# Second tiles for raw weights and weight parts, and part stores issued from ScalarE

## The chip, the cores and the metric

The kernel runs on one core of a Trainium2 chip. The metric is device time in microseconds (us), the median over runs of the whole program. Times inside the program are counted from its first profiled instruction.

## The reference

Three computations follow each other. The first is an attention in two steps: 32 packed queries per head attend to keys and values, and the 576 queries of each of 8 batches attend to that packed result, in 8 heads of 64. The second and third are products with weights, over 4608 tokens:

```python
a = x @ w1
b = x @ w2
h = a * b @ w3
x = h @ w_out                     # 512 wide again
h = x @ w_in                      # 512 -> 2048
g = where(h >= 1, h, where(h <= -1, 0, (h + 1) ** 2 / 4))
out = g @ w_out2                  # 2048 -> 512
```

The weights arrive as 64-bit floats.

## The kernel before

The kernel has three stages. In the first (to about 170 us) the weights of the second computation are read and converted, and the attention of batches 0 and 1 is done. In the second stage a loop over batches b = 1 to 7 (line 675) multiplies batch b with its weights, while the attention of batch b + 1 is spread over the same instructions. In the third stage (from about 654 us, line 803 on) the third computation runs over nine blocks of tokens.

One batch of the second stage is 24 units, u = 0 to 23: sixteen `ab_unit` (line 367, 12 matmuls on L377 each) and eight `x2_unit` (line 413, 24 matmuls on L401 each). Behind each unit come up to two more things, in this order: a step of the next batch's attention (the list EARLY and LATE, lines 39 and 40, say behind which units), and in batches 1 to 6 one weight task, taken from the list `w_todo` (lines 699 to 702). The order in which the code emits instructions is the order on each engine.

The weight tasks prepare the weights of the third stage: 32 blocks of 128x512 64-bit words (16 of `win`, 16 of `wout`). A conversion task (`w_convert`, line 572) turns a raw block in SBUF into 32-bit floats (ScalarE L123, VectorE L128, L130, L134), and then issues the load of the next raw block from SyncE's queue (`load_weight`, line 106, L109). There is one raw tile (`bufs=1`). A part task (`w_parts`, line 581) splits one converted block into a rounded high part (ScalarE L585) and the rest (GpSimd L586), and issues the store of both, 512 KB, to DRAM from SyncE's queue (L587). The two parts lie in one tile `hl`, of which there is one (`bufs=1`). A combining task (L591) adds or subtracts two converted blocks on GpSimd. A line of tasks always takes three units, and a part task is always its first: parts start at units that are multiples of 3. There are 44 part tasks and 138 tasks with the empty ones. The third stage reads the stored parts back (`wi_load`, `wo_load`).

SyncE's queue also holds the large attention loads: the queries of the next batch are issued behind u = 3 (`load_q`, L157), the values and the small packed queries of the batch after behind u = 10 (`load_v`, L168 and L169, `load_p`, L162), the keys behind u = 14 (`load_k`, L152). Each load stands ahead of the weight task of the same unit. ScalarE's queue already issues the stores of the second stage's results (L429, 72 of them).

The conversions fall behind these units (b.u): 1.0, 1.1, 1.2, 1.3, 1.20, 1.22; 2.1, 2.2, 2.4, 2.7, 2.10, 2.13; 3.5, 3.7, 3.10, 3.11, 3.13, 3.16, 3.19, 3.22; 4.14, 4.16, 4.19, 4.20, 4.22; 5.1, 5.4, 5.7, 5.23; 6.1, 6.4, 6.5.

Of the kernel before, what the change touches and what calls it, by code (L numbers as in the profile page):

```python
# [8 lines left out]
F32 = mybir.dt.float32  # L9
F32R = mybir.dt.float32r  # L10
# [12 lines left out]
P = 128  # L23
# [33 lines left out]
def fused_kernel(ctx: ExitStack, tc, qT, kT, vv, pb, w1, w2, w3T, wo, win, wout, out):  # L57
    nc = tc.nc
# [22 lines left out]
    cv = tc.alloc_tile_pool(name="cv0", bufs=1, side="left", reuse_waits="tile")  # L81
# [24 lines left out]
    def load_weight(pool, src, bufs=1):  # L106

        t = pool.tile([P, 512], src.dtype, name="raw", tag="raw", bufs=bufs)
        nc.sync.dma_start(out=t, in_=src)  # L109
        return t  # L110

    def as_float32(pool, raw, out, bufs=1):

        if raw.dtype == F32:
            return lambda: None, lambda: None, lambda: nc.vector.tensor_copy(out=out, in_=raw)
        quarters = raw.bitcast(U16).rearrange("p (n four) -> p n four", four=4)
        t = pool.tile([P, 512], F32, name="cvt", tag="cvt", bufs=bufs)
        halves = out.bitcast(U16).rearrange("p (n two) -> p n two", two=2)  # L120

        def scale():
            nc.scalar.activation(  # L123
                out=t, in_=raw.bitcast(F32).rearrange("p (n two) -> p n two", two=2)[:, :, 1],
                func=AF.Copy, scale=2.0 ** -112)

        def parts():
            nc.vector.tensor_scalar(  # L128
                out=halves[:, :, 0], in0=quarters[:, :, 1], scalar1=13, scalar2=None, op0=ALU.logical_shift_right)
            nc.vector.tensor_scalar(  # L130
                out=halves[:, :, 1], in0=quarters[:, :, 3], scalar1=0x8000, scalar2=None, op0=ALU.bitwise_and)

        def join():
            nc.vector.scalar_tensor_tensor(  # L134
                out=out.bitcast(I32), in0=t.bitcast(I32), scalar=3, in1=out.bitcast(I32),
                op0=ALU.logical_shift_left, op1=ALU.bitwise_or)
        return scale, parts, join
# [214 lines left out]
    def emit(step):  # L352
        pe, ew = step
        if pe:
            pe()
        ew()
# [77 lines left out]
    raw = {}  # L434
# [120 lines left out]
    cv = tc.alloc_tile_pool(name="cv1", bufs=1, side="left", reuse_waits="tile")  # L555
# [9 lines left out]

    wx = {}
    w_todo = []

    def w_raw(src):
        raw["w"] = load_weight(cv, src)  # L570

    def w_convert(key, nxt):
        def f():
            x = wx[key] = cv.tile([P, 512], F32, name="cvx", tag="cvx", bufs=4)
            for f in as_float32(cv, raw.pop("w"), x):
                f()
            if nxt is not None:
                w_raw(nxt)
        return f

    def w_parts(key, dst):
        def f():
            x = wx[key]
            p = cv.tile([P, 2, 512], F32R, name="hl", tag="hl", bufs=1)
            nc.scalar.activation(out=p[:, 0], in_=x, func=AF.Copy)  # L585
            nc.gpsimd.tensor_tensor(out=p[:, 1], in0=x, in1=p[:, 0].bitcast(F32), op=ALU.subtract)  # L586
            nc.sync.dma_start(out=dst, in_=p.bitcast(F32))  # L587
        return f

    def w_combine(key, a, b, op):  # L590
        return lambda: nc.gpsimd.tensor_tensor(out=wx[key], in0=wx[a], in1=wx[b], op=op)  # L591

    def weight_tasks():

        groups = [(k, n) for n in range(2) for k in range(2)]
        seq = []
        for x, (k, n) in enumerate(groups):
            for r, c in ((0, 0), (1, 1), (1, 0), (0, 1)):
                seq.append(win[(2 * c + k) * P:(2 * c + k + 1) * P, (2 * r + n) * 512:(2 * r + n + 1) * 512])
            for j in range(4 * x, 4 * x + 4):  # L600
                r = (j % 2) * 8 + j // 2
                seq.append(wout[r * P:(r + 1) * P, :])
        conv = [lambda: w_raw(seq[0])]
        nxt = seq[1:] + [None]
        conv = []
        for x in range(4):
            for q in (11, 22, 21, 12):
                conv.append(w_convert((x, q), nxt[len(conv)]))
            for j in range(4 * x, 4 * x + 4):
                conv.append(w_convert(("o", j), nxt[len(conv)]))  # L610
        lines = [[conv.pop(0) for _ in range(3)], [conv.pop(0)]]
        for x, (k, n) in enumerate(groups):
            q = {z: (x, z) for z in (11, 12, 21, 22)}
            take = lambda m=1: [conv.pop(0) for _ in range(m) if conv]
            part = lambda i, z: w_parts(q[z], wid[i][n][:, k])
            lines.append([part(A11, 11), None, None])
            lines.append([part(A22, 22), w_combine(q[22], q[21], q[22], ALU.add), None])
            lines.append([part(A12, 12), None, None])
            lines.append([part(S1, 22), w_combine(q[22], q[22], q[11], ALU.subtract),
                          w_combine(q[21], q[11], q[21], ALU.subtract)])  # L620
            lines.append([part(S2, 22), w_combine(q[12], q[12], q[22], ALU.subtract)] + take())
            lines.append([part(S3, 21)] + take())
            lines.append([part(S4, 12)] + take() + take())
            for j in range(4 * x, 4 * x + 4):
                lines.append([w_parts(("o", j), wod[j // 2][:, j % 2])] + take())
        out = []
        for l in lines:
            out += (l + [None, None, None])[:3]
        assert not conv
        w_raw(seq[0])  # L630
        return out

    raw.clear()
    w_todo += weight_tasks()
    assert len(w_todo) <= 144, len(w_todo)

    wi_t, wo_t = {}, {}

    def wi_load(i, n):
        t = wi_t[i, n] = late["b1" if i in LEFT else "b2"].tile([P, 2, 2, 512], F32R, name=f"wi{i}{n}")  # L640
        nc.sync.dma_start(out=t.bitcast(F32), in_=wid[i][n])
# [4 lines left out]
    def x2_load(t):  # L646
        f = late["b1"].tile([P, 4, TB], F32, name="f", tag="f", bufs=1)
        t0 = t * TB
        nc.sync.dma_start(out=f, in_=x2d[t0 // XD][:, :, t0 % XD:t0 % XD + TB])
        for r in range(2):  # L650
            for c in range(2):
                x2f[10 * r + c + 11] = f[:, 2 * r:2 * r + 2, c * TH:(c + 1) * TH]
# [12 lines left out]
    def x2_tasks(t):  # L665

        return [
            x2_parts(t, A11, 11), x2_combine(11, 12, 11), x2_combine(12, 22, 12),
            x2_parts(t, S1, 11), x2_parts(t, A12, 21),
            x2_parts(t, S4, 22), x2_combine(22, 22, 11),  # L670
            x2_parts(t, S2, 22), x2_combine(21, 21, 22),
            x2_parts(t, S3, 12), x2_parts(t, A22, 21),
        ]

    for b in range(1, B):
        if b + 1 < B:
            att, sa, bm = attention(b + 1)
            spread = dict(zip(EARLY, att))
            spread.update(zip(LATE, [bm[1, 0], bm[0, 0], sa[0], sa[1], bm[1, 1], bm[0, 1]]))
        else:  # L680
            spread = {}
            b1 = late["b1"] = tc.alloc_tile_pool(name="b1", bufs=1, side="left", reuse_waits="tile")
            x2_load(0)
            for n in range(2):
                for i in LEFT:
                    wi_load(i, n)
            x2_todo = x2_tasks(0)
        seq = []
        for f, n in ((ab_unit, 8), (x2_unit, 4)):
            seq += [f(b, mt, hf) for hf in range(2) for mt in range(n)]  # L690
        for u, unit in enumerate(seq):
            emit(unit)
            if u in spread:
                emit(spread[u])
            if b == B - 1:
                for _ in range(2 if u >= 18 else 0):
                    if x2_todo:
                        x2_todo.pop(0)()
            elif w_todo:
                task = w_todo.pop(0)  # L700
                if task:
                    task()
        if b == B - 2:
            cv.release()
            a2.release()
# [205 lines left out]
```

## Time and profile before

| what | value |
|---|---|
| median of 3 runs | 1424.65 us (1422.08 to 1431.35) |
| the profiled execution | 1425.31 us |
| its span, first to last instruction | 1423.5 us |
| TensorE (PE) busy | 1335.9 us, 94% of the span |
| VectorE (DVE) busy | 801.6 us, 56% |
| ScalarE (ACT) busy | 618.3 us, 43% |
| GpSimd (POOL) busy | 129.4 us, 9% |
| mean granted TensorE clock, as a share of full speed | 0.978 |

The profiled execution lies within the spread of the runs. Its span leaves 1.8 us around the program's instructions. A busy matmul can be a slowed one: busy time alone doesn't say that TensorE ran at its peak.

### The profile page before, as it was taken

To read this page: it belongs to the slowest core of one execution; us is meant where nothing else is said; L and a number is where in the kernel's file an instruction comes from. 1 tells how busy PE (TensorE), PEld (TensorE's weight loads), DVE (VectorE), ACT (ScalarE), POOL (GpSimd) and SP (SyncE) were. 2 spreads that over 40 slices of the span, in tenths; PEclk is the share of its full clock that TensorE was granted. 3 is DMA by queue.
4 is the path that set the end of the run, shared out by engine and by line. 5 is a ranking of instruction groups with operands and counts; after the bars stand their busy time and mean duration, and the time that the engine had idled before them with its cause. 6 is when DMAs were issued, how large, how long until landed. Compare 5 with 4: busy or idle time off the path is not lost.

```text
span 1423.5 us, 23629 instructions
## 1 busy us (share of the span) xinstructions
PE 1335.9 (94%) x9576; PEld 1163.8 (82%) x9576; DVE 801.6 (56%) x1480; ACT 618.3 (43%) x1272; POOL 129.4 (9%) x102
## 2 busy tenths in 40 slices
PE   6689789889699999999999999999999999999998
PEld 2367678778588888898988989898898989989897
DVE  4784556655556665534555555656555555555553
ACT  3344243434254534334344444544444453444533
POOL 0000012112012121001000000001000000100000
PEclk9899999999799999999999999999999999999999
DMA  9762445544445544347324243333434233242332
GB/s 280 238 227 92 142 145 155 184 156 166 152 159 180 201 149 160 126 181 302 141 96 167 93 148 119 119 123 115 148 111 153 93 131 136 93 174 89 126 111 89
DMA packets 58878, 212.56 MB, mean 149 GB/s; under 512 B 5777, under 2 KB 17041, under 8 KB 45713
## 3 DMA queue, kind: packets, MB, share of 16 engines
q1 hardware_dynamic: 43216, 190.99, 39.0%
q10 hardware_dynamic: 15552, 20.06, 3.9%
q8 instruction: 75, 1.23, 0.4%
q14 instruction: 35, 0.28, 0.1%
HBM read 167.90 MB, written 43.12 MB: 148 GB/s over the span
## 4 chain that ended last, share of the span: by engine, by line
PE 68%; DVE 11%; DMA 10%; ACT 5%; issue 2%; POOL 1%; SPq 1%; ACTq 1%; DVEq 0%; POOLq 0%
PE o L795 24%; PE x L765 13%; PE psk L401 9%; PE psk L377 9%; PE z L765 6%; PE y L765 3%; DMA raw<-wout 2%; DMA wi<-hl 2%; DMA raw<-w3T 2%; DMA raw<-win 1%; PE psk L193 1%; DVE g L103 1%; PE psk L485 1%; DMA wo<-hl 1%; ACT r L778 1%
## 5 line engine op out<-in xcount | busy, mean ns | idle before, releaser
L795 PE MATMUL o<-wo,g 128*128 128x512 f32 x1728 | 441.3, 391 | 1.3 <-ACT g L102 1.3
L795 PEld LDWEIGHTS o<-wo,g 128*128 128x128 f32 x1728 | 304.7, 188 | 48.5 <-ACT g L102 1.7
L765 PEld LDWEIGHTS x<-x2s,wi 128*128 128x128 f32 x1728 | 243.2, 189 | 36.4 <-ACT m L773 12.4
L765 PE MATMUL x<-x2s,wi 128*128 128x256 f32 x1728 | 252.1, 282 | 7.7 <-ACT m L773 5.3
L401 PEld LDWEIGHTS psk<-g,w 128*128 128x128 f32 x1500 | 206.9, 194 | 36.9 <-ACT st L428 24.6
L401 PE MATMUL psk<-g,w 128*128 128x288 f32 x1500 | 215.2, 303 | 12.9 <-ACT st L428 8.4
L377 PE MATMUL psk<-at,m 128*128 128x288 f32 x1494 | 217.6, 302 | 5.7 <-DVE at L328 1.9
L377 PEld LDWEIGHTS psk<-at,m 128*128 128x128 f32 x1494 | 203.9, 191 | 20.9 <-issue 8.6
L779 DVE TENSOR_TENSOR H<-H,r 128x512 f32<-128x512 f32 x144 | 99.7, 692 | 182.5 <-ACT r L778 182.5
L102 ACT ACTIVATE g<-H 128x512 fp32r<-128x512 f32 x144 | 90.6, 629 | 108.6 <-DVE H L780 108.4
L778 ACT ACTIVATE r<-H,half 128x512 f32<-128x512 f32 x144 | 104.2, 724 | 66.3 <-DVE H L831 64.0
L765 PE MATMUL z<-x2s,wi 128*128 128x256 f32 x864 | 125.0, 281 | 0.0
L103 DVE TENSOR_TENSOR g<-H,g 128x512 fp32r<-128x512 f32 x144 | 103.6, 720 | 29.8 <-ACT g L102 29.8
L655 POOL TENSOR_TENSOR f<-f 128x512 f32<-128x512 f32 x36 | 49.2, 1367 | 699.9 <-DVE x2s L662 698.5
L765 PEld LDWEIGHTS z<-x2s,wi 128*128 128x128 f32 x864 | 112.0, 191 | 0.0
L389 DVE TENSOR_TENSOR tb<-psk,ta 128x288 f32<-128x288 f32 x124 | 56.4, 455 | 90.5 <-ACT ta L387 42.2
L586 POOL TENSOR_TENSOR hl<-cvx,hl 128x512 fp32r<-128x512 f32 x44 | 57.5, 1307 | 498.9 <-ACT hl L585 266.5
L780 DVE SCALAR_TENSOR_TENSOR H<-r,H 128x512 f32<-128x512 f32 x144 | 99.7, 692 | 4.9
L123 ACT ACTIVATE cvt<-raw 128x512 f32<-128x512 f32 x72 | 48.6, 678 | 89.3 <-DMA raw<-wout 31.3
L103 DVE TENSOR_TENSOR g<-tb,g 128x288 fp32r<-128x288 f32 x128 | 74.7, 583 | 17.5 <-ACT g L102 16.8
L485 PE MATMUL psk<-wo,w3f 128*128 128x512 f32 x128 | 61.9, 636 | 14.2 <-DVE w3f L134 14.2
L662 DVE TENSOR_TENSOR x2s<-f,x2s 128x512 fp32r<-128x512 f32 x63 | 46.8, 765 | 37.7 <-ACT x2s L661 37.7
(85 smaller groups left out, 1122.1 us busy)
## 6 DMA issues: line engine op xcount, KB each, us to landing
wo<-wo SPq DMA_DIRECT2D x72, 1024.0 KB, 4.8
wi<-hl SPq DMA_DIRECT2D x28, 512.0 KB, 2.6
wi<-wi SPq DMA_DIRECT2D x14, 1024.0 KB, 6.9
x2d<-st ACTq DMA_DIRECT2D x72, 144.0 KB, 1.8
qk<-kT SPq DMA_DIRECT2D x8, 1152.0 KB, 7.0
qk<-qT SPq DMA_DIRECT2D x8, 1152.0 KB, 5.9
f<-x2d SPq DMA_DIRECT2D x9, 1024.0 KB, 7.5
out<-st ACTq DMA_DIRECT2D x36, 256.0 KB, 2.7
```

The source lines that it names most:

```text
L102: nc.scalar.activation(out=dst[:, 0], in_=src, func=AF.Copy)
L103: nc.vector.tensor_tensor(out=dst[:, 1], in0=src, in1=dst[:, 0].bitcast(F32), op=ALU.subtract)
L377: nc.tensor.matmul(ps[w][:, :HS], m_tile[b, w, n][:, s, G, c0 * P:(c0 + 1) * P], at_tile[b][:, G, v, hf * HS:(hf + 1) * HS], start=(k == 0 ...
L389: nc.vector.tensor_tensor(out=g, in0=ps[0][:, :HS], in1=bs, op=ALU.mult)
L401: nc.tensor.matmul(ps, w34[kt][:, s, mt * P:(mt + 1) * P], g_t[kt, hf][:, v, :], start=(kt == kts[0] and n == 0), stop=(kt == kts[-1] and ...
L485: nc.tensor.matmul(acc[4 * hf + m], w3f[hf, j][:, m * P:(m + 1) * P], wof[j], start=(j == 0), stop=(j == 7))
L586: nc.gpsimd.tensor_tensor(out=p[:, 1], in0=x, in1=p[:, 0].bitcast(F32), op=ALU.subtract)
L765: nc.tensor.matmul(bank[b], wi_t[q, n][:, k, s, c0 * P:(c0 + 1) * P], x2_t[t, q][:, v, k, :], start=(j == 0 and q in (A11, S1, A12)), stop ...
L778: nc.scalar.activation(out=r, in_=src, func=AF.Relu, scale=0.5, bias=half)
L779: nc.vector.tensor_tensor(out=src, in0=src, in1=r, op=ALU.max)
L780: nc.vector.scalar_tensor_tensor(out=src, in0=r, scalar=1.0, in1=src, op0=ALU.min, op1=ALU.mult)
L795: nc.tensor.matmul(acc[c], g2_t[t, i, h][:, s, c * P:(c + 1) * P], wo_t[i][:, h, v, :], start=(i == 0 and h == 0 and n == 0), stop=(i == 7 ...
```

## The change

The raw block and the part tile get two tiles each. The first two raw blocks are loaded at the start, and each conversion issues the load of the block after the next. The store of a part is not issued by the part task, but put on a list; one unit later, behind that unit's attention step and ahead of its weight task, it is issued from ScalarE's queue. The 8 KB per partition that this takes come from a smaller scratch for dynamic DMAs.

```diff
-    def w_raw(src):
-        raw["w"] = load_weight(cv, src)
+    w_stores = []
+    raws = []
 
     def w_convert(key, nxt):
         def f():
             x = wx[key] = cv.tile([P, 512], F32, name="cvx", tag="cvx", bufs=4)
-            for f in as_float32(cv, raw.pop("w"), x):
+            for f in as_float32(cv, raws.pop(0), x):
                 f()
             if nxt is not None:
-                w_raw(nxt)
+                raws.append(load_weight(cv, nxt, 2))
 
     def w_parts(key, dst):
         def f():
             x = wx[key]
-            p = cv.tile([P, 2, 512], F32R, name="hl", tag="hl", bufs=1)
+            p = cv.tile([P, 2, 512], F32R, name="hl", tag="hl", bufs=2)
             nc.scalar.activation(out=p[:, 0], in_=x, func=AF.Copy)
             nc.gpsimd.tensor_tensor(out=p[:, 1], in0=x, in1=p[:, 0].bitcast(F32), op=ALU.subtract)
-            nc.sync.dma_start(out=dst, in_=p.bitcast(F32))
+            w_stores.append(lambda: nc.scalar.dma_start(out=dst, in_=p.bitcast(F32)))
...
-        conv = [lambda: w_raw(seq[0])]
-        nxt = seq[1:] + [None]
+        nxt = seq[2:] + [None, None]
...
-        w_raw(seq[0])
+        for src in seq[:2]:
+            raws.append(load_weight(cv, src, 2))
...
             elif w_todo:
+                for f in w_stores:
+                    f()
+                w_stores.clear()
                 task = w_todo.pop(0)
...
-    nc = bacc.Bacc("TRN2", target_bir_lowering=False, num_devices=1)
+    nc = bacc.Bacc("TRN2", target_bir_lowering=False, num_devices=1, dynamic_dma_scratch_size=4096)
```

## Rows read from the trace of the kernel before

**Rows 1.** Batches 1 to 6: length, busy PE, PEld, DVE, ACT, POOL; clock; DMA share, GB/s.
```profile
172.05:249.70 77.65, 67.79 (x591) 59.89 (x590) 49.00 (x95) 33.29 (x75) 13.57 (x10) 0.93 0.47 148
249.70:324.29 74.59, 64.94 (x590) 57.00 (x589) 42.55 (x86) 31.73 (x73) 11.66 (x9) 0.98 0.49 172
324.29:404.87 80.58, 65.54 (x590) 57.95 (x589) 46.16 (x91) 32.88 (x75) 14.70 (x11) 0.89 0.47 159
404.87:473.47 68.60, 65.54 (x589) 58.20 (x589) 42.99 (x83) 31.47 (x72) 16.04 (x12) 0.95 0.52 172
473.47:537.75 64.28, 62.77 (x590) 55.60 (x589) 39.68 (x79) 30.37 (x70) 15.54 (x12) 1.00 0.53 175
537.75:603.34 65.59, 63.22 (x590) 55.64 (x589) 38.68 (x77) 29.36 (x69) 8.01 (x6) 1.00 0.38 135
```

**Rows 2.** TensorE's timeline, its idle times of batches 1 to 6.
```profile
192.29 1.96 PE L232 MATMUL psm<-ident,big 128*116 128x128 f32 x8 [4.55 <-ACT big L216]
...
236.14 4.76 PE L401 MATMUL psk<-g,w 128*128 128x288 f32 x24 [2.57 <-ACT st L428]
...
264.12 1.09 PE L232 MATMUL psm<-ident,big 128*116 128x128 f32 x8 [2.30 <-ACT big L216]
...
297.35 8.03 PE L401 MATMUL psk<-g,w 128*128 128x288 f32 x48 [4.48 <-ACT ta L387]
...
312.06 3.44 PE L401 MATMUL psk<-g,w 128*128 128x288 f32 x24 [1.26 <-ACT st L428]
...
369.29 1.22 PE L193 MATMUL psm<-qk,ppt 64*32 64x288 f32 x16 [15.04 <-DVE big L295]
...
458.77 5.92 PE L401 MATMUL psk<-g,w 128*128 128x288 f32 x24 [3.06 <-ACT st L428]
...
525.52 3.44 PE L401 MATMUL psk<-g,w 128*128 128x288 f32 x24 [1.51 <-ACT st L428]
```

**Rows 3.** All engines' timeline, ScalarE's waits for a raw block or a part tile.
```profile
188.19 0.68 ACT L123 ACTIVATE cvt<-raw 128x512 f32<-128x512 f32 x1 [3.24 <-DMA raw<-win]
...
227.39 0.63 ACT L585 ACTIVATE hl<-cvx 128x512 fp32r<-128x512 f32 x1 [7.83 <-DMA wi<-hl]
...
270.69 0.64 ACT L585 ACTIVATE hl<-cvx 128x512 fp32r<-128x512 f32 x1 [2.05 <-DMA wo<-hl]
...
296.33 0.67 ACT L123 ACTIVATE cvt<-raw 128x512 f32<-128x512 f32 x1 [10.14 <-DMA raw<-win]
...
366.05 0.67 ACT L123 ACTIVATE cvt<-raw 128x512 f32<-128x512 f32 x1 [15.42 <-DMA raw<-wout]
```

**Rows 4.** The same timeline, SyncE's queue around the value load of batch 2.
```profile
278.31 4.82 SPq L169 DMA_DIRECT2D v<-vv  x1
...
283.98 0.49 SPq L109 DMA_DIRECT2D raw<-win  x1
```

**Rows 5.** All instructions on L169 (values): issue time in ns, time to landing.
```profile
L169 SPq DMA_DIRECT2D v<-vv x8: 2852/4648/4863, 18.8 to 497.6; - x8
...
DMA to landing us min/median/max: 16.3/18.8/20.4
```

**Rows 6.** Instructions on the tile hl: durations in ns, minimum, median and maximum.
```profile
L585 ACT ACTIVATE hl<-cvx x44: 612/623/635, 196.6 to 578.4; 128x512 fp32r<-128x512 f32 x44
L586 POOL TENSOR_TENSOR hl<-cvx,hl x44: 1274/1290/1579, 197.3 to 579.1; 128x512 fp32r<-128x512 f32 x44
...
DMA to landing us min/median/max: 2.6/2.7/12.0
```

**Rows 7.** All instructions on L429 (stores from ScalarE's queue).
```profile
L429 ACTq DMA_DIRECT2D x2d<-st x72: 326/326/760, 98.5 to 654.6; - x72
...
DMA to landing us min/median/max: 1.7/1.8/7.9
```

**Rows 8.** The queues' timeline around the first value load of batch 1.
```profile
102.59 4.86 SPq L169 DMA_DIRECT2D v<-vv  x1
...
106.90 0.33 ACTq L429 DMA_DIRECT2D x2d<-st  x1
```

## The prediction

> **What bounds the kernel now.** TensorE is busy for 94% of the span, so the first question is where the rest is. A table by stretch, cut at the first matmul of each batch, answers it [rows 1]. The least disturbed batch, the fifth, takes 64.28 us, and TensorE is busy for 62.77 us of it at full clock. Batch 3 holds the same matmuls and takes 80.58 us, 65.54 of it busy, at a granted clock of 0.89: there TensorE waits, and some of its busy time is slowed. I take 62.77 us as what a batch needs. The excess is then, from batch 1 to 6: 14.9, 11.8, 17.8, 5.8, 1.5 and 2.8 us, together 54.6 us. That is all that a change to the weight tasks can win: the matmuls stay as they are.
>
> The second view, TensorE's own timeline, says where the excess sits [rows 2]. Nearly all idle times are put down to ScalarE or VectorE, but these are only the messengers. ScalarE's timeline shows what they waited for [rows 3]: in batch 3 ScalarE stands 15.42 us for a raw block, and TensorE idles 15.04 us. In batch 2 it stands 10.14 us for a raw block, and TensorE idles 4.48 and then 1.26 us. In batch 1 it stands 7.83 us for the one part tile, whose store has not landed, and TensorE idles 2.57 us. A conversion or part task thus stands in ScalarE's order ahead of the copies that free TensorE's PSUM banks.
>
> The third view, SyncE's queue, says why the data is late. In batch 2 the load of values is issued at 278.31 us, its issue alone takes 4.82 us, and the raw block for the conversion at u = 13 is issued behind it at 283.98 us [rows 4]. It can be used at 296.33 us [rows 3]. The values take 16.3 to 20.4 us from issue to landing [rows 5], and what stands behind them in the queue lands with them. The stores of parts go the same way: typically 2.7 us, up to 12.0 us [rows 6].
>
> **The change part by part. Raw blocks one step earlier.** Each conversion uses a block whose load was issued two conversions before it, not one. I went through the list of tasks with this rule.
>
> Batch 1, units 0 to 3: four conversions follow each other, and the third stands 3.24 us for its block [rows 3]. The first two blocks are now loaded ahead, the third is issued one unit earlier: the wait goes. Of the idle 4.55 us behind it [rows 2] I count 2.7, since VectorE's work for the maximum of the scores follows at its own pace. The eight transposes after it took 1.96 us where those after 264.12 us took 1.09 [rows 2]: 0.9 more; for the slowed matmuls behind them I estimate twice that, 1.9. That makes 5.5 us.
>
> Batch 2: the conversion at u = 13 now uses a block issued at u = 7, ahead of the values. What goes is 4.48 us, 1.26 us, and 1.5 us of slowed matmuls (8.03 us for 48, where two times 3.44 for 24 make 6.9, and 0.4 taken for those before them), 7.2 us in sum [rows 2]. The early waits of the batch go too: 2.30 us [rows 2], and about 1.6 us of two shorter ones behind the part tile's wait of 2.05 us [rows 3]. Together 11.1 us.
>
> Batch 3: the conversion at u = 11 uses a block issued at u = 7, ahead of the values, so the 15.04 us go, and with them an estimated 2.0 us of slowed matmuls, since the clock of this batch was the lowest [rows 1], 17.0 us in all. But the next conversion, at u = 13, uses a block issued at u = 10, behind the values. That is the geometry of batch 2 before the change, so I put back its price, 7.2 us. Net 9.8 us.
>
> Batch 4: the conversion at u = 14 issues its load behind the keys, but that block is now wanted at u = 19, not at u = 16. Idle 3.06 us, and 24 matmuls in 5.92 us where 3.44 are usual [rows 2]: 5.5 us go, to which the part tile contributes.
>
> Batches 5 and 6: 1.5 us behind a wait for the part tile [rows 2], and in batch 6 the conversions at u = 4 and 5 stand close together: 2.4 of its 2.8 us.
>
> The loads are the same in number and size; 32 of them only move.
>
> **Two part tiles.** A tile is wanted again six units after its part task instead of three: 16 us at 64.28 us for 24 units [rows 1], though the shorter units come closer. With the 12.0 us of the slowest store [rows 6] nearly all such waits go. Their effect is counted in the batches above, and in batch 1 it is 4 us more: 2.57 us idle, and 1.3 us of the 4.76 us for 24 matmuls [rows 2].
>
> The sum is 5.5 + 4 + 11.1 + 9.8 + 5.5 + 1.5 + 2.4 = 39.8 us.
>
> **The stores on ScalarE's queue.** 44 store issues leave SyncE's queue, where they took as long as on ScalarE's, and where the raw, value, query and key loads stood behind their wait for GpSimd. ScalarE's issue takes 0.33 us [rows 7], so ScalarE has 44 x 0.33 = 14.5 us more to do in 430 us. What hides it is its idle time: it is busy for 30 to 33 us of each batch [rows 1]. The store also waits for GpSimd, whose subtraction takes 1.29 us behind ScalarE's copy [rows 6]. It is issued one unit later, and ahead of it stand that unit's own copies and attention step. Queued behind it on ScalarE are the conversion of the same unit and the copies of the next, and TensorE waits for these through its banks. From below this costs nothing, or gains a little where the values are issued sooner. From above, every store shows with 1.29 + 0.33 us, 71 us in all. I take 2 us, near the lower end, because a part task precedes each store by a whole unit, and even the shorter units have twelve matmuls, 1.7 us at 3.44 us for 24 [rows 2], more than the 1.29 us.
>
> A rule of the Trainium skill speaks against this part: "DMA: Bandwidth & Descriptors", section "Issuing engines are not separate DMA queues", says that transfers issued from different engines end up on the same DMA engines, so that another issuing queue saves issue time only. The trace partly agrees: a 144 KB store from ScalarE's queue typically lands in 1.8 us, but in up to 7.9 us [rows 7]. By the rule alone the moved stores land no sooner, and the second tile has to do the whole work; that is the second rival.
>
> **The scratch** issues no instruction; I cost it at nothing. Where the tiles lie moves by some KB, and a load could meet another tile's release: not seen in any row, 0 to 2 us, and I take 1 us for it and all else. With 2 us for the stores the net gain is 37 us. The profiled execution took 1425.31 us, 0.7 us above the median, so both references agree: 1425.3 - 37 gives 1388 us.
>
> **The rivals.** *The issue of the values holds ScalarE's store.* In each of batches 1 to 5 the store of the part of u = 9 comes up at u = 10, just when SyncE spends 4.6 us on issuing the values [rows 5]. If one issue excludes the other, ScalarE stands for up to 4.6 us five times. Waits of that size cost TensorE about 3 us (10.14 us cost 5.7 in idle time): 15 us, 1403 us. Against it: a ScalarE issue at 106.90 us lies inside a SyncE issue from 102.59 to 107.45 us and took the usual 0.33 us [rows 8]. "Perfetto Trace Analysis" of the Trainium skill, section "DMA Instruction — HWDGE (DVE, Sync)", describes such a lock on a shared descriptor generator; the row doesn't show one. 12%.
>
> *The stores land late and the waits for the part tile stay.* Beside the values a store shares their engines. If the store of u = 10 is not landed at u = 15, batches 1 to 5 keep a wait there; at up to the 4 us of batch 1, and 1.5 to 4 in the others, that is 14 us: 1402 us. For it: the 7.9 us of a much smaller store [rows 7]. Against it: the store has five units to land. 13%.
>
> *The third batch's wait goes too,* because SyncE issues the values sooner when no store stands before them: 7.2 us more, 1381 us. 8%.
>
> *ScalarE becomes the bound, and the kernel slower.* The store waits at the head of ScalarE's order while PSUM copies stand behind it. If all 44 show with 1.29 + 0.33 us, 71 us come on top of the 39.8 won: 1456 us. From (39.8 + 14) / 44 = 1.2 us per store on it is slower by over 1%. For it: the same messenger role of ScalarE that costs so much now. Against it: half of each batch is idle time of ScalarE. 4%.
>
> *The change does not do what it says:* the added tiles wait for their place, or the blocks stay late because the queue itself is full. Then nothing much moves, 1420 us. 4%.
>
> **How the numbers follow.** The forecast has 59%. Its own spread, from errors of the terms, is 1380 to 1396 us. The range reaches to the third batch's case below (with the remaining excess, 1425 - 54.6 = 1371 us is the floor) and to both rivals near 1403 us above: 1375 to 1405 us. Within 1%, about what a measurement can tell from no change, means 14 us: all up to 1410 us is faster. Forecast, the two rivals near 1403 and the third batch's case hold 92%; some of the two rivals, if they come together, falls into the middle. Faster 0.88, same 0.08, slower 0.04.
>
> **What would show it.** In the profile of the changed kernel batch 2 should take about 63 to 65 us, batch 3 about 70 us with one wait for a raw block at u = 13, and batch 1 about 68 us. Waits of ScalarE for the tile hl should be nearly gone. The 44 stores should show on ScalarE's queue with 0.33 us each; an issue of several us at u = 10 would show the first rival, a wait for the tile at u = 15 the second. The third stage (from 654 us on) should keep its length. The prediction is wrong if batches 2 and 3 don't shorten, or if new waits behind the stores on ScalarE come up in all six batches.

## The result and the profile after

The changed kernel takes 1390.71 us (median of 4 runs, 1388.27 to 1395.25) beside 1426.22 us of the kernel before in the same comparison: a ratio of 0.9753, with a 95% interval of 0.971 to 0.9796. Forecast were 1388 us. Its profiled execution has a span of 1386.5 us, 37.0 us less than before.

Busy time by batch, cut at the first matmul of each batch as in [rows 1] (columns: stretch, length, busy PE, PEld, DVE, ACT, POOL; clock; DMA share, GB/s):

```profile
174.55:242.19 67.64, 63.65 (x591) 55.80 (x590) 47.73 (x94) 32.56 (x75) 13.59 (x10) 1.00 0.52 177
242.19:305.81 63.62, 63.12 (x590) 55.55 (x589) 42.31 (x86) 32.03 (x73) 11.61 (x9) 1.00 0.59 201
305.81:377.61 71.80, 65.46 (x589) 58.05 (x589) 45.56 (x91) 32.84 (x75) 14.56 (x11) 0.95 0.53 179
377.61:440.31 62.70, 62.70 (x589) 55.59 (x589) 41.97 (x83) 31.48 (x72) 15.91 (x12) 1.00 0.56 188
440.31:503.00 62.69, 62.69 (x589) 55.58 (x589) 38.89 (x79) 30.23 (x70) 15.51 (x12) 1.00 0.54 179
503.00:565.71 62.71, 62.71 (x590) 55.60 (x589) 38.62 (x77) 29.66 (x69) 7.92 (x6) 1.00 0.38 132
```

In the last three batches TensorE is busy from the first matmul to the last, at full clock (granted clock 1.00). Batch 3 is the only one that still stands out. From first to last matmul cut the six batches took 431.3 us before and take 391.2 now: 40.1 us less. The span shows 37.0 of it, because the first batch starts 2.5 us later (174.55 us against 172.05) and the part behind batch 6 is 0.6 us longer. The later start is probably spread: the changed kernel run once more started its first batch at 176.0 us, and the other kernels of the table below with the same loads of values and the smaller scratch between 173.6 and 177.5 us. The kernel before was profiled once, so how far its own start moves is not shown.

TensorE's own timeline of the changed kernel, three of the seven idle times that its six batches have left (the other four are at most 1.66 us each):

```profile
191.39 1.09 PE L232 MATMUL psm<-ident,big 128*116 128x128 f32 x8 [1.50 <-ACT big L216]
...
349.03 9.02 PE L401 MATMUL psk<-g,w 128*128 128x288 f32 x48 [4.47 <-ACT ta L387]
...
365.36 3.44 PE L401 MATMUL psk<-g,w 128*128 128x288 f32 x24 [1.87 <-ACT st L428]
```

The first answers to 192.29 us in [rows 2]: 1.50 us idle instead of 4.55, and the eight transposes take 1.09 us instead of 1.96. The 15.04 us of batch 3 are gone; in their place stand 4.47 and 1.87 us, the pattern that batch 2 had before. The timeline of all engines shows what is behind it:

```profile
327.02 5.02 SPq L169 DMA_DIRECT2D v<-vv  x1
...
328.63 0.33 ACTq L586 DMA_DIRECT2D wi<-hl  x1
...
332.96 16.30 SPq L109 DMA_DIRECT2D raw<-win  x3
...
348.01 0.67 ACT L123 ACTIVATE cvt<-raw 128x512 f32<-128x512 f32 x1 [9.96 <-DMA raw<-win]
```

The second of the two loads of values (L169) is issued from 327.02 us on, the raw block for u = 13 behind them at 332.96, and ScalarE stands 9.96 us for it. The second line is a store of parts on ScalarE's queue. It is issued in the middle of the values' issue, and takes 0.33 us.

In the changed kernel the line numbers of the part task are one lower than before: ScalarE L584, GpSimd L585, store L586. ScalarE's waits from 165 us on, that is, from the table of who waited for whom (us in total, times, longest), the lines on the raw tile and the part tile, first of the kernel before, then of the changed one:

```profile
ACT cvt L123 <- DMA raw<-wout: 31.3, 7, 15.4
...
ACT hl L585 <- DMA wi<-hl: 24.9, 6, 7.8
...
ACT cvt L123 <- DMA raw<-win: 16.8, 6, 10.1
...
ACT hl L585 <- DMA wo<-hl: 6.6, 4, 3.5
```

```profile
ACT cvt L123 <- DMA raw<-win: 10.0, 1, 10.0
...
ACT cvt L123 <- POOL hl L585: 8.3, 8, 1.2
ACT ta L387 <- POOL hl L585: 7.5, 7, 1.2
```

Before, that makes 48.1 us of waits for raw blocks, in 13 pieces, and 31.5 us for the part tile, in 10. One raw wait is left, none for the part tile. New are 15.8 us in which a store on ScalarE's queue waits for GpSimd, with whoever stands behind it.

### The profile page after: what moved, and what is told of

The parts are those of the page before. It is cut to its first block, busy times and chain, and to the rows that moved or that the text cites. A ratio compares the mean times of both kernels' runs of the same rounds, so it can differ in the third digit from the quotient of the medians.

```text
span 1386.5 us, 23532 instructions
## 1 busy us (share of the span) xinstructions
PE 1327.9 (96%) x9576; PEld 1156.6 (83%) x9576; DVE 797.9 (58%) x1480; ACT 617.8 (45%) x1272; POOL 129.0 (9%) x102
## 3 DMA queue, kind: packets, MB, share of 16 engines
q1 hardware_dynamic: 36880, 167.92, 35.5%
## 4 chain that ended last, share of the span: by engine, by line
PE 77%; DVE 9%; DMA 6%; ACT 4%; issue 2%; POOL 1%; ACTq 0%; SPq 0%; DVEq 0%; POOLq 0%
PE o L797 24%; PE x L767 13%; PE psk L401 13%; PE psk L377 12%; PE z L767 6%; PE y L767 3%; DMA raw<-w3T 2%; PE psk L193 2%; DVE x2s L661 1%; DMA raw<-win 1%; PE psk L485 1%; PE psm L182 1%; ACT r L780 1%; DVE g L103 1%; DMA st<-x2d 1%
## 5 line engine op out<-in xcount | busy, mean ns | idle before, releaser
L401 PEld LDWEIGHTS psk<-g,w 128*128 128x128 f32 x1500 | 203.3, 191 | 30.2 <-ACT st L428 16.2
L401 PE MATMUL psk<-g,w 128*128 128x288 f32 x1500 | 211.7, 300 | 6.3 <-ACT ta L387 4.5
L377 PE MATMUL psk<-at,m 128*128 128x288 f32 x1494 | 213.7, 298 | 3.6 <-DVE m L103 1.7
L377 PEld LDWEIGHTS psk<-at,m 128*128 128x128 f32 x1494 | 200.6, 188 | 17.8 <-issue 7.2
L585 POOL TENSOR_TENSOR hl<-cvx,hl 128x512 fp32r<-128x512 f32 x44 | 57.4, 1305 | 461.1 <-DVE g L103 234.6
L387 ACT ACTIVATE ta<-psk 128x288 f32<-128x288 f32 x125 | 50.6, 405 | 49.8 <-PE psk L377 40.1
L103 DVE TENSOR_TENSOR g<-tb,g 128x288 fp32r<-128x288 f32 x128 | 69.8, 545 | 3.5 <-ACT g L102 2.8
```

The costliest lines, as they stand in the source:

```text
L103: nc.vector.tensor_tensor(out=dst[:, 1], in0=src, in1=dst[:, 0].bitcast(F32), op=ALU.subtract)
L377: nc.tensor.matmul(ps[w][:, :HS], m_tile[b, w, n][:, s, G, c0 * P:(c0 + 1) * P], at_tile[b][:, G, v, hf * HS:(hf + 1) * HS], start=(k == 0 ...
L401: nc.tensor.matmul(ps, w34[kt][:, s, mt * P:(mt + 1) * P], g_t[kt, hf][:, v, :], start=(kt == kts[0] and n == 0), stop=(kt == kts[-1] and ...
```

## The experiments

The table gives the length of each batch in the profiled execution of each kernel, from its first L377 matmul to the next batch's (us; such a cut lies up to 0.2 us from the one above), and the ratio to the kernel before. Kernels were compared with runs of the kernel before on the same chip, so ratios are compared, not times: the kernel before took 1426.22 us in the first comparison, 1421.67 us beside e0 to e3, 1420.88 beside e4 to e7 and 1424.26 beside e8 to e11.

| kernel | start of b1 | b1 | b2 | b3 | b4 | b5 | b6 | ratio (95% interval) |
|---|---|---|---|---|---|---|---|---|
| before | 172.1 | 77.5 | 74.6 | 80.6 | 68.6 | 64.3 | 65.6 | 1 |
| changed | 174.6 | 67.5 | 63.6 | 71.8 | 62.7 | 62.7 | 62.7 | 0.9753 (0.971 to 0.9796) |
| e0_scratch | 174.1 | 73.0 | 73.8 | 79.8 | 68.6 | 64.9 | 65.1 | 1.0012 (0.999 to 1.0034) |
| e1_raw2 | 177.0 | 69.2 | 68.9 | 72.0 | 63.9 | 63.9 | 62.7 | 0.986 (0.9838 to 0.9882) |
| e2_hl2 | 174.1 | 73.4 | 74.4 | 78.9 | 63.0 | 62.7 | 66.2 | 0.9948 (0.9928 to 0.9968) |
| e3_act_store | 175.7 | 72.4 | 73.0 | 75.6 | 64.7 | 64.7 | 66.5 | 0.9971 (0.9948 to 0.9994) |
| e4_sp_late | 173.6 | 67.8 | 63.1 | 71.7 | 62.7 | 62.7 | 62.7 | 0.9756 (0.9729 to 0.9783) |
| e5_act_now | 177.5 | 68.2 | 68.1 | 76.5 | 64.0 | 65.1 | 65.5 | 0.9924 (0.99 to 0.9948) |
| e6_raw3 | 173.7 | 67.9 | 63.6 | 63.2 | 62.7 | 62.7 | 62.7 | 0.9719 (0.9694 to 0.9745) |
| e7_vsplit | 155.2 | 67.8 | 63.6 | 63.1 | 62.7 | 62.7 | 62.7 | 0.9593 (0.9569 to 0.9617) |
| e8_raw3_vsplit | 161.8 | 67.7 | 63.6 | 62.8 | 62.7 | 62.7 | 62.7 | 0.9574 (0.9534 to 0.9614) |
| e9_before_vsplit | 157.5 | 72.1 | 67.3 | 71.8 | 62.7 | 63.2 | 65.2 | 0.9715 (0.9673 to 0.9757) |
| e10_sp_now | 175.7 | 67.8 | 63.1 | 73.4 | 62.7 | 62.7 | 62.7 | 0.9774 (0.9736 to 0.9813) |
| e11_after | 176.0 | 67.8 | 63.6 | 73.5 | 62.7 | 62.7 | 62.7 | 0.9772 (0.9729 to 0.9815) |

### One part of the change at a time

The theory (A) was that the late raw blocks had cost most, the rival (B) that the part tile and the queue of its store had.

**e1_raw2**, against the changed kernel:

```diff
-            p = cv.tile([P, 2, 512], F32R, name="hl", tag="hl", bufs=2)
+            p = cv.tile([P, 2, 512], F32R, name="hl", tag="hl", bufs=1)
...
-            w_stores.append(lambda: nc.scalar.dma_start(out=dst, in_=p.bitcast(F32)))
+            nc.sync.dma_start(out=dst, in_=p.bitcast(F32))
```

> One part of the change alone: two raw tiles; one part tile, and its store at once from SyncE's queue, as before. Theory A (the late raw blocks carried most of the gain): batch 2 falls from 74.6 to about 65 us, batch 3 from 80.6 to about 72, batches 4 and 5 keep their waits for the part tile (about 67 and 64); sum about 25 of the 37 us, so about 1400 us. Theory B (the part tile and the queue of its store carried it): at most 12 us, 1414 us or more, and ScalarE's waits for raw blocks stay, since stores still stand before the loads.

It took 1399.85 us beside 1421.67: 1.4%, more than half of the whole gain. Batches 2 and 3 by the table of stretches:

```profile
246.30:315.10 68.80, 63.29 (x588) 55.51 (x588) 42.87 (x86) 31.83 (x73) 11.66 (x9) 1.00 0.57 186
315.10:387.10 72.00, 65.06 (x589) 57.65 (x588) 45.81 (x91) 32.79 (x75) 14.79 (x11) 0.95 0.52 178
```

Batch 3 has the length of the changed kernel, so two raw tiles do all of that batch. Batch 2 stays 5 us longer, and not at 65 us as expected: with the raw wait gone the one part tile holds ScalarE instead (36.8 us of waits for it in the six batches, where the kernel before had 31.5). Batch 4 fell further than expected, to 63.9 us instead of 67; batch 5 took the 64 us expected.

**e2_hl2**, against the changed kernel: one raw tile (`seq[1:]`, `seq[:1]` and 1 in place of `seq[2:]`, `seq[:2]` and 2), and the store as before:

```diff
-                raws.append(load_weight(cv, nxt, 2))
+                raws.append(load_weight(cv, nxt, 1))
...
-            w_stores.append(lambda: nc.scalar.dma_start(out=dst, in_=p.bitcast(F32)))
+            nc.sync.dma_start(out=dst, in_=p.bitcast(F32))
```

> One part alone: two part tiles; one raw tile, stores at once from SyncE's queue. Theory A: only the part tile's waits go, 4 us in batch 1, 1 in batch 2, 3 to 4 in batch 4, 1.5 in batch 5: about 10 us, 1416 us; batch 3 stays at 80 us. Theory B: 25 us or more, 1400 us or less.

It took 1412.88 us: 0.5%. Batches 3 and 4:

```profile
321.80:400.80 79.00, 64.11 (x590) 56.50 (x589) 46.17 (x91) 32.85 (x75) 14.56 (x11) 0.91 0.47 162
400.80:463.70 62.90, 62.71 (x588) 55.53 (x588) 41.33 (x80) 31.37 (x72) 16.09 (x12) 1.00 0.51 180
```

Batch 3 stays long, as theory A had it; batch 4 is cured whole, 5.6 of its 5.9 us. e1 took 4.7 us off the same batch with the other part. In the kernel before, the two waits stand in series there: 6.08 us for the part tile up to 448.77 us, 1.61 us for a raw block up to 452.72. That shortening either lets TensorE's lead cover the other fits both runs, but is argued and not shown. In batch 1 the 4 us that theory A expected are not shown either: e2 takes 73.4 us there, and e0 below, the kernel before with the smaller scratch, 73.0.

**e3_act_store**, against the changed kernel: one raw tile and one part tile, the store a unit later from ScalarE's queue.

> One part alone: the stores go out a unit later from ScalarE's queue; one raw tile and one part tile. Theory A: the raw waits of 10 and 15 us in batches 2 and 3 stay (75 and 80 us), the stores land sooner than behind the values (after the whole change at most 7.8 us, before 12.0), so most waits for the part tile go though there is one: 5 to 10 us, about 1418 us. Theory B, in the form that the queue itself was the trouble: the raw loads come sooner too, 20 us or more, 1405 us or less. A third possibility, that the store's wait for GpSimd holds ScalarE: slower than 1426 us.

It took 1416.04 us, 0.3%, at the lower end of what theory A expected. Batch 3 falls by 5 us, since SyncE no longer stands for GpSimd and issues the values 21.1 us into the batch (342.09 us) instead of 23.8 (347.87 us); the raw wait there is 11.1 us instead of 15.4. SyncE's queue, first in the kernel before, where a store waits for GpSimd up to 347.40 us, then in e3:

```profile
347.43 0.32 SPq L587 DMA_DIRECT2D wi<-hl  x1
347.87 0.28 SPq L168 DMA_DIRECT2D v<-vv  x1
```

```profile
342.09 0.27 SPq L168 DMA_DIRECT2D v<-vv  x1
```

Neither the strong form of B nor a slower kernel came.

**e0_scratch**, against the kernel before:

```diff
-    nc = bacc.Bacc("TRN2", target_bir_lowering=False, num_devices=1)
+    nc = bacc.Bacc("TRN2", target_bir_lowering=False, num_devices=1, dynamic_dma_scratch_size=4096)
```

> The kernel before with the smaller scratch alone. Expected by all theories: no change, 1426 us within 2 us. If the 2.5 us by which the first batch starts later after the change (174.55 us against 172.05) come from where tiles lie, this run shows a start near 174.5 us and up to 2.5 us more; if they are spread between executions, it need not.

No change in time (1421.94 us beside 1421.67). Its first batch started at 174.1 us, which fits either reading of the later start. Its batch 1 came out 4.5 us shorter than before in the profiled execution, with the same instructions: single batches of single executions differ by some us, and only the ratios decide about those.

### Does the queue of the store matter?

**e4_sp_late**, against the changed kernel:

```diff
-            w_stores.append(lambda: nc.scalar.dma_start(out=dst, in_=p.bitcast(F32)))
+            w_stores.append(lambda: nc.sync.dma_start(out=dst, in_=p.bitcast(F32)))
```

> The whole change, but the stores, still a unit later, go out from SyncE's queue. If ScalarE's queue mattered (a store issued at u = 10 now stands behind the values and is wanted free again at u = 15), ScalarE waits for the part tile at u = 15 again, up to 7 us in batches 1 to 5, and the kernel takes about 1396 to 1402 us. If the two tiles alone do the work, it takes the changed kernel's 1391 us within 3 us.

**e10_sp_now**: the same line as `nc.sync.dma_start(out=dst, in_=p.bitcast(F32))` in the part task itself. Beside it on the same chip ran the changed kernel again, **e11_after**.

> Two raw tiles and two part tiles, and the store at once from SyncE's queue as before: the change without the later store and without ScalarE's queue. If the two tiles do the work: the changed kernel's time within 3 us (e4, the store a unit later from SyncE, has shown the queue to be of no account). If SyncE's standing for GpSimd ahead of the loads matters: 5 us or more slower than the changed kernel.

> The changed kernel once more, beside the other runs on one chip: a ratio of 0.975 to the kernel before, 1386 to 1391 us; its first batch starts at 173 to 177 us as in the other runs, since that start differs from execution to execution.

Ratios of 0.9756, 0.9774 and 0.9772: the changed kernel without its new queue, and without the later store either, is as fast. (The 1386.13 us of e4 lie below the range expected, as the kernel before was faster on that chip too; the ratio is that of the first comparison.) ScalarE's waits of e4_sp_late from 165 us on:

```profile
ACT cvt L123 <- DMA raw<-win: 8.4, 1, 8.4
...
ACT hl L584 <- DMA wo<-hl: 0.2, 1, 0.2
```

A store of e4 lands after up to 11.2 us, one of the changed kernel after up to 7.8 (below), and it makes no difference: the second tile alone takes the wait away. In e10 no wait for the part tile is left either, and its one raw wait is 10.2 us. So, as far as intervals of about 0.4% tell, the two tiles are the whole effect of the change. e11 repeats the ratio of the first comparison (0.9753) within its interval, and also its one raw wait, 10.2 us.

```profile
L586 ACTq DMA_DIRECT2D wi<-hl x28: 326/326/327, 196.9 to 515.7; - x28
...
L586 ACTq DMA_DIRECT2D wo<-hl x16: 326/326/327, 256.4 to 544.1; - x16
...
DMA to landing us min/median/max: 2.6/3.6/7.8
```

These are the stores of the changed kernel, by their line (durations in ns: minimum, median, maximum). All took the usual 0.33 us to issue, also those in the middle of the values.

**e5_act_now**, against the changed kernel:

```diff
-            w_stores.append(lambda: nc.scalar.dma_start(out=dst, in_=p.bitcast(F32)))
+            nc.scalar.dma_start(out=dst, in_=p.bitcast(F32))
```

> The whole change, but the store is issued at once in the part task from ScalarE's queue, so that ScalarE stands for GpSimd's 1.29 us at each of the 44 stores instead of 0 to 1.2 us. If ScalarE's idle time hides it, as the forecast's 2 us for the stores had it: 1391 to 1394 us. If each store shows: 44 x about 1.3 us, up to 1448 us.

It took 1408.94 us where e4 beside it took 1386.13: 22.8 us more, 0.52 us per store, between the two expectations. ScalarE's waits from 165 us on:

```profile
ACT ta L387 <- POOL hl L585: 28.8, 16, 1.8
...
ACT st L428 <- POOL hl L585: 7.5, 4, 1.9
```

These are 36.3 us instead of the 15.8 us of the changed kernel, and they stand ahead of the copies that free TensorE's banks: even batches 4 to 6, with no late data, take 64.0 to 65.5 us. A wait on ScalarE is not hidden just because ScalarE is idle for half of the time. What hides it in the changed kernel is the unit in between: its 15.8 us of such waits leave TensorE without idle time in batches 4 to 6.

### The wait that is left

**e6_raw3**: three raw tiles (`seq[3:]`, `seq[:3]` and 3).

> The changed kernel with three raw tiles. The block for u = 13 of batch 3 is then issued at u = 7, ahead of the values; the one for u = 16 is issued at u = 10 behind them and is wanted some 10 us later. Theory A (the one wait left, 9.96 us, is this late block): batch 3 falls from 71.8 to 63 to 66 us, the kernel to about 1383 us (1381 to 1386). If batch 3's length has another cause, it stays at 1391 us.

It took 1379.72 us, a ratio of 0.9719. Batch 3:

```profile
305.20:368.30 63.10, 62.72 (x589) 55.54 (x588) 45.64 (x91) 32.85 (x75) 14.55 (x11) 1.00 0.61 203
```

8.6 us less than in the changed kernel, at full clock and with hardly an idle time. The block behind the values was the cause. The whole kernel lies below the 1381 to 1386 us expected, but the kernel before was faster on this chip too: beside the 1386.13 us of e4 it won 6.4 us, where about 8 were expected.

**e7_vsplit**, against the changed kernel:

```diff
-        nc.sync.dma_start(out=t[:, :n], in_=vv[b, :n * CH].rearrange("(c p) d -> p c d", p=CH))
+        rows = vv[b, :n * CH].rearrange("(c p) d -> p c d", p=CH)
+        nc.sync.dma_start(out=t[:112, :n], in_=rows[:112])
+        nc.sync.dma_start(out=t[112:, :n], in_=rows[112:])
```

> The changed kernel with the main load of values (116 partitions) issued as two loads, of 112 and of 4 partitions. Theory: the values land late (16 to 20 us) because a load of 116 partitions is spread over few DMA engines, and the raw block behind them waits for that. Then they land in about 7 to 10 us, like the 1152 KB of keys (7.0 us), ScalarE's wait of 9.96 us in batch 3 falls to 0 to 2 us, and the kernel takes about 1383 us. If it is the number of short rows that makes the load slow, nothing changes: 1391 us, landing 16 us or more.

It took 1361.93 us beside 1420.88, a ratio of 0.9593: the fastest kernel of this study, together with e8 below. The loads of values by line, first of the changed kernel (L169 is its second load, of 112 partitions, which stands behind the one of 116), then of e7 (L169 of 112, L170 of 4, L171 the second load):

```profile
L169 SPq DMA_DIRECT2D v<-vv x8: 2576/4691/5827, 18.4 to 461.5; - x8
...
DMA to landing us min/median/max: 16.9/18.0/18.1
```

```profile
L169 SPq DMA_DIRECT2D v<-vv x8: 328/329/430, 18.1 to 433.5; - x8
L170 SPq DMA_DIRECT2D v<-vv x8: 270/390/442, 18.5 to 433.9; - x8
L171 SPq DMA_DIRECT2D v<-vv x8: 323/323/1136, 19.0 to 434.3; - x8
...
DMA to landing us min/median/max: 6.6/7.8/8.6
```

The traces hold these landings for three of the eight second loads of the changed kernel and for five of e7. The same bytes in rows of the same length land in 7.8 us instead of 18.0, and the issue that took 4.7 us takes 0.3. The DMA packets in the traces show the difference: the values of a batch are 576 packets of 2 KB, of which 4 to 6 are under way on average while they load in the changed kernel, and 13 to 17 in e7; the last one ends 14 to 21 us after the first load's issue, and 7 to 12 us in e7. So it was not the number of rows. Whether another split would do as well was not run. Batch 3 falls to 63.1 us, as with three raw tiles. The rest of the gain I had not expected: the first stage, which loads the values of two batches, ends 19 us earlier in this execution (155.2 us; e8 and e9, with the same split, end it at 161.8 and 157.5). The stretch up to the first batch, first of the changed kernel, then of e7:

```profile
0.00:174.55 174.55, 139.93 (x918) 89.33 (x919) 105.02 (x231) 64.14 (x124) 0.70 (x6) 0.93 0.61 195
```

```profile
0.00:155.20 155.20, 134.27 (x919) 85.93 (x919) 104.82 (x230) 63.85 (x123) 0.70 (x6) 0.99 0.66 220
```

**e8_raw3_vsplit** has both edits, **e9_before_vsplit** the split load alone in the kernel before.

> Three raw tiles and the split load of values, on top of the change. Theory (both remove one and the same wait in batch 3): batch 3 is 63.1 us with either already, so nothing more is to be had: 1362 us, as with the split alone, within 2 us. If they remove different waits: some 7 us less, 1355 us.

> The kernel before with the split load of values and nothing of the change. Theory (the slow landing of the values makes the raw blocks late, and one tile each then doesn't suffice): the first batch starts 19 us earlier, and batches 2 and 3 fall to about 65 to 67 us, since a raw block waits at most 3 to 5 us behind values that land in 7.8; with the part tile's waits shortened too, about 1380 us, so that 15 to 20 of the change's 35 us are left to win by it. If one tile each is the trouble by itself, batches 2 and 3 stay at 72 us or more and the kernel takes 1400 us.

e8 took 1361.68 us, a ratio of 0.9574 where e7 has 0.9593: no more than their intervals allow, so both edits remove one and the same wait. e9 took 1382.91 us, beside 1424.26. On top of the split load the deeper tiles of e8 are thus still worth about 21 us (1382.91 against 1361.68 on the same chip); for the change itself, with two raw tiles, it is the step from 0.9715 to 0.9593. But batch 3 of e9 takes 71.8 us, and not 65 to 67. Its timeline:

```profile
322.88 0.42 SPq L109 DMA_DIRECT2D raw<-wout  x1
...
331.52 0.66 ACT L123 ACTIVATE cvt<-raw 128x512 f32<-128x512 f32 x1 [8.79 <-DMA raw<-wout]
```

A raw block issued right behind values that land in some 8 us is still 8.6 us away, and wanted one unit later. Fast values shorten the wait from 15.4 to 8.8 us; only the earlier issue removes it. Both reasons given in the expectation hold in part.

## Why the prediction was right

**The size of what could be won** was read from the table of stretches: 62.77 us as the need of a batch, 54.6 us of excess. The changed kernel's batches 4 to 6 take 62.7 us. The step holds.

**The raw blocks.** By batch the prediction took off 9.5, 11.1, 9.8, 5.5, 1.5 and 2.4 us (in batch 1 with the 4 us of the part tile), 39.8 in sum; measured are 10.0, 11.0, 8.8, 5.9, 1.6 and 2.9, 40.1 in sum (the first with the spread of some us that e0 shows for batch 1). Following the list of tasks with the rule that a conversion uses the block issued two conversions before it found the one wait that remains, at u = 13 of batch 3, and its origin. Its price, taken from batch 2 before the change, was 7.2 us; by the table of stretches it is 71.80 - 62.70 = 9.1 us, of which e6 took 8.6 off. So the sum came out right, but in part by luck. The 4 us for the part tile in batch 1 were read from one execution, in which ScalarE stood 7.83 us for that tile and TensorE 2.57 us behind it. In e0, with the same instructions, ScalarE's wait at that place is half as long, and TensorE's timeline has no idle time behind it:

```profile
225.09 0.63 ACT L585 ACTIVATE hl<-cvx 128x512 fp32r<-128x512 f32 x1 [3.99 <-DMA wi<-hl]
```

Against e0 the six batches of the changed kernel are 34.2 us shorter, not 40.1, and batch 1 is shorter by 5.5 us, what the prediction took off for its raw blocks alone (each of these is one execution). By this reading the forecast of the whole, 37 us beside 35.5 between the medians, is as close as it is because the 3 us taken off for costs, which no run shows, nearly make up for these 4 us: without either the sum is 35.8 us.

The prediction also read L169 as the load of values. It is the second and smaller one; its long issue and late landing [rows 4, 5] came from the load in front of it, as e7 shows, where they go away with that load split. What it drew from them, that the raw block behind lands late, holds.

**Who won it where** was partly wrong. The prediction counted batch 4 with the raw blocks, "to which the part tile contributes"; the part tile alone wins 5.6 us there (e2), the raw tile alone 4.7 (e1), so that the two can't be added. And parts were added as if independent: in batch 2 the raw tile alone wins 5.7 us, the part tile alone 0.2, both together 11.0. The parts of the change one by one won 1.4, 0.5 and 0.3%, together 2.2, where the whole wins 2.5; the intervals do not separate these two.

**The stores on ScalarE's queue** were taken at 2 us, with two reasons: a unit lies between, and ScalarE is idle for half of each batch. The cost is not to be seen (batches 4 to 6 have no idle time of TensorE, and e4 and e10 without it are no faster). e5 shows that only the first reason was good: without the unit in between 44 stores cost 22.8 us, against the same idle ScalarE. This is also the mechanism of the rival that ends slower. Its point of decision was 1.2 us per store; even at once it shows with 0.52.

**The queue itself** wins nothing: 0.9756 from SyncE a unit later, 0.9753 from ScalarE; and on one chip 0.9774 from SyncE at once, 0.9772 from ScalarE later. The runs agree with the rule quoted from the Trainium skill ("DMA: Bandwidth & Descriptors", section "Issuing engines are not separate DMA queues"), by which another issuing queue saves issue time only.

**The other rivals.** That the issue of the values holds ScalarE's store: the store at 328.63 us, inside the values' issue, took 0.33 us, and all 44 took 326 to 327 ns. The section that the prediction named for such a lock, "DMA Instruction — HWDGE (DVE, Sync)" of "Perfetto Trace Analysis" in the Trainium skill, speaks of a generator shared by VectorE and SyncE, not of ScalarE. That stores land late and waits at u = 15 stay: no wait for the tile is left. That batch 3's wait goes too: it needed e6 or e7. The 1 us for the scratch and all else is not to be seen: e0 finds no change (1.0012, 0.999 to 1.0034). The 2.5 us by which the first batch started later are probably the spread of that start.

## What to carry to other kernels

A wait is shown at the engine that stands, but it is made where the load was issued: for each consumer write down which load it uses, where that was issued and what large transfer stands between, and a deeper set of tiles can be priced stretch by stretch before it is built. Before giving a late transfer more lead, look at the load it stands behind: splitting that one load alone won 2.9% here (e9; of its profiled execution 14.6 us in the first stage), the deeper tiles 2.5%, both together over 4%. A store that waits for another engine does not belong right behind its producer on an engine that others wait for; with one unit of other work in between no cost was to be seen here.

## What the runs showed of the hardware that was not expected

A load of 928 KB to 116 partitions, with a small one behind it, took 18.0 us to land, and the issue of the next load on the same queue up to 5.8 us. As 112 and 4 partitions it took 7.8 us, and no issue of values more than 1.2 us. The Trainium skill, "DMA: Bandwidth & Descriptors", section "Why a DMA increments its semaphore by 16 and not by 1", has a rule that fits: the number of DMA engines that share such a load is the largest up to 16 that divides the partition count, which is 4 for 116 and 16 for 112. The traces agree: 4 to 6 packets of the values are under way on average before the split, 13 to 17 after it. They do not name the engine of a packet.

A store on ScalarE's queue was not held by a 5.0 us issue on SyncE's queue that was under way.
